# Scores of three batches kept in SBUF, and the state rows' second layer in seven half-block products

## Chip, core and metric

One core of a Trainium2 chip runs the whole kernel. The metric is device time of the launch in microseconds, lower is better. The engines that matter are TensorE (PE in the profile; its weight loads are PEld), VectorE (DVE), ScalarE (ACT), GpSimd (POOL, here only a queue of casting loads) and SyncE (SP, the queue of the stores).

## What is computed

Two blocks follow each other. The first is attention between a sequence and a small state, in both directions; the second is a feed-forward layer with a squared ReLU on every row that the first gives.

```
B, H, S, Ns, D = 8, 8, 512, 32, 64
scores  = scale * x @ state^T          # 512 x 32 for each batch and head
xread   = softmax(scores) @ state      # the sequence reads the state
scores2 = scale * state @ x^T          # the same products, transposed
sread   = softmax(scores2) @ x         # the state reads the sequence
rows    = concat(xread, sread)         # 544 rows per batch, 512 wide
h       = rows @ w_in                  # 512 -> 2048, "layer one"
out     = (s * max(h, 0)^2 + b) @ w_out  # 2048 -> 512, "layer two"
```

So there are 8 x 512 sequence rows and 8 x 32 state rows. The 256 state rows of all batches go through the feed-forward layer together, at the very end.

## The kernel before

**One batch.** `at_xT` (DVE) transposes the batch's rows in 32x32 squares into `xT`. `at_T` (PE) makes the scores `T` of all eight heads in one PSUM tile of two banks (128 partitions x 1024 fp32) with 16 small matmuls that use the array in 32x32 tiles. From `T` two chains start. The first, for the sequence's softmax, is `at_U` (DVE transpose out of PSUM), `at_mu` (maximum), `at_D` (subtract), `at_E1` (exponential on ACT), `at_z`, `at_At`, `at_A`. The second, for the state's softmax, is `at_nm` (DVE maximum of `T`), `at_E2` (two exponentials of `T` on ACT, with their sums), `at_a2`, `at_a2T` (a transpose through PE, `aps`, and a copy back), `at_V` (PE, into `vps`), `at_srd` (an ACT copy into `srdT`, which gathers the state rows of all batches).

The product with the state is folded into `w_in`: `at_M` makes `M = state @ w_in` per batch in four units of 512 columns (`mps`), `at_Mc` copies each to SBUF. Layer one is then `M` against `A`, two matmuls for each of the 16 slices of 128 hidden columns (`layer1_x`, PSUM tile `hps`, two buffers), followed by ReLU on ACT and a square on DVE (`square`, two slices at a time) into `g`. Layer two is `g` against `w_out`.

**The order** is written out by hand: the program does not reorder anything, and each engine executes its list in the order of the calls. A piece for the first batch and a half stands as straight code (L583 to L671). Then come eight calls of `phase`, for b = 0 to 7. Phase b runs layer one of batch b+1 (in phase 7: of the state rows, `sr`) in 16 steps, and layer two of batch b among them. Lists `before` and `behind` hold pairs of a step number and a piece of work that goes ahead of or behind that step's layer one. `chain(b+2, ...)` puts the first softmax chain of the batch after next there.

For batches 3 to 7 both chains start from one `T`. For batches 0, 1 and 2 the first chain has to run early, in the straight code and in phase 0; the second runs late: `late(2, ...)` in phase 3, `late(0, ...)` and `late(1, ...)` in phase 6. Each `late` begins with a second `at_T` of the same batch. (Batch 0 makes its first `T` in two halves of the sequence, in two PSUM tiles, and each half has its own `at_U`.) For that the `xT` of batches 0 to 2 is kept in buffers of their own; the other batches share one.

**Layer two of batches 6 and 7** (`fast_layer2`) is split in 2x2 blocks and done with seven block products in place of eight: DVE makes sums of blocks of `g` (S1 to S4, in place or in `S3`) and, once for the kernel, differences of blocks of `w_out` (`T1` to `T4` of `weight_sum`). The PSUM tile X collects four products and is read out (`evict`) between them; Y holds one, W two. A product is two pieces of eight matmuls of 256 columns, u = 0 to 13, one per step, with step 8 left free: u = 13 stands at step 14, the last eviction and its four DMAs (`put`) behind step 15.

**The end** is layer two of the 256 state rows: 128 rows in 16 matmuls of 512 columns, evicted and stored as one; then the other 128 rows in two halves of 16 matmuls of 256 columns, each evicted (L821) and stored (L824). Both halves lie in one PSUM bank.

In PSUM (eight banks) there are four pairs of banks: `pt` and `pa` (tiles of two banks, shared by `T`, `mps`, `aps`, `vps` in turn), `ph` for layer one and `po` for layer two.

Of the kernel before, what the change touches and what calls it, by code (L numbers as in the profile page):

```python
# [15 lines left out]
def kernel(  # L16
# [12 lines left out]
    nc = tc.nc  # L29
# [138 lines left out]
    def w_out_f(f):  # L168
        return w_out16[:, f, :]
# [58 lines left out]
    def at_xT(b, g=None, p=None):  # L228

        if "xT" not in at[b]:  # L230
            keep = b < 3
            at[b]["xT"] = (konst if keep else apool).tile(
                [P, NG, S, 2], FP16, name=f"xT_{b}", tag=f"xTk{b}" if keep else "xT"
            )
        out = at[b]["xT"].rearrange("p g s e -> p g (s e)").bitcast(FP32)
        in_ = xh_t[b].rearrange("p g j d -> p g (j d)").bitcast(FP32)
        nc.vector.transpose(part(out, p, g), part(in_, p, g))  # L237

    def at_T(b, p=None):

        half = p is not None
        at[b]["T"] = T = two_banks(f"T_{b}", own=not p)
        for e in range(2):
            for hp in range(4):
                for g in range(NG):
                    r = hp ^ g
                    mm(
                        part(T[Ns * hp : Ns * hp + Ns], p, g)[:, 0, :],
                        stE[32 * r : 32 * r + 32, NG * b + g, :, e],
                        part(at[b]["xT"][32 * r : 32 * r + 32, :, :, e], p, g)[:, 0, :],  # L250
                        start=(e == 0), stop=(e == 1),
                        tp=(32 * r, Ns * hp),
                    )

    def at_U(b, p=None, g=None):
        U = sm(b, "U", [P, NG, S], FP32)
# [48 lines left out]

    def at_nm(b):
        nm, nms = sm(b, "nm", [P, NG], FP32), sm(b, "nms", [P, NG], FP32)
        nc.vector.tensor_reduce(  # L308
            nm, at[b]["T"], AX.X, ALU.max, negate=True
        )  # L310
        nc.vector.tensor_scalar(nms, nm, scale, None, ALU.mult)  # L311

    def at_E2(b, gs=range(NG)):
        E2, rs = sm(b, "E2", [P, NG, S], FP16), sm(b, "rs", [P, NG], FP32)
        for g in gs:
            nc.scalar.activation(  # L316
                E2[:, g], at[b]["T"][:, g], AF.Exp,
                bias=at[b]["nms"][:, g : g + 1], scale=scale, accum_out=rs[:, g : g + 1],
            )

# [61 lines left out]
        at_Mc(b, j, copy)  # L382


    G_t, R_t = {}, {}

    def new_G(tag, ntok):
        if tag not in G_t:
            G_t[tag] = gpool.tile([P, NKF, S], FP16, name=f"g_{tag}", tag="g")[:, :, :ntok]
        return G_t[tag]  # L390

    def layer1(tag, f, terms, ntok):
# [78 lines left out]
        }[name]()  # L471
        nc.vector.tensor_sub(T[name], a, b)

    def fast_layer2(b):
# [47 lines left out]
        def put(i, rr):  # L522
# [11 lines left out]
            ("W", lambda: A(0, 1), orig(1, 1), False, True),  # L534
            ("X", lambda: A(1, 1), summed("T4"), False, True),
        ]
        out = [(u + u // 8, lambda u=u: product(*products[u // 2], u % 2)) for u in range(14)]
        out += [(0, lambda: s3(1)), (0, lambda: s1(1)), (1, lambda: evict(top, 0, "X")), (1, lambda: s2(0))]
        out += [(2, lambda: s2(1)), (3, lambda: evict(top, 0, "Y", True))]
        out += [(5, lambda: s4(0)), (6, lambda: evict(top, 1, "X")), (6, lambda: s4(1))]  # L540
# [8 lines left out]
        return [lambda: s3(0), lambda: s1(0)], out  # L549

    def spread_scalars():
        sps = two_banks("sbps")[:, 0, 0:2]
# [121 lines left out]
    def phase(tag, before, behind):  # L674
        for i in range(NKF):
            for when, piece in before:
                if when == i:
                    piece()
            if tag == "sr":
                layer1_sr(i)  # L680
            else:
                layer1_x(tag, i)
            if i and i % 2 == 0:
                square(tag, i - 2)
            for when, piece in behind:
                if when == i:
                    piece()
        square(tag, NKF - 2)

    def chain(b, s):  # L690
        return [
# [60 lines left out]
    for b in range(0, B):  # L752
        if b in fast:
            before, behind = [], fast[b]
        else:
            before, behind = l2(b, 3 if b == 1 else 0) if b else ([], first())
        if b in (2, 4):
            for i, name in enumerate(("T1", "T2") if b == 2 else ("T3", "T4")):
                before += [(12 + 2 * i + h, lambda h=h, name=name: weight_sum(name, h)) for h in range(2)]
        behind = left + behind  # L760
        if b + 1 in FAST:
            sums, fast[b + 1] = fast_layer2(b + 1)
            before += [(14 + i, p) for i, p in enumerate(sums)]
        if b + 3 < B:
            before += [(2 if b else 5, lambda b=b: load_x(b + 3))]
        if b + 3 < B:
            before += [(13, lambda b=b: at_xT(b + 3))]
        if b and b + 2 < B:
            before += [(7, lambda b=b: load_xn(b + 2))]
        if b == B - 3:  # L770
            before += [(9, lambda: load_xn(0))]
        if b == B - 2:
            before += [(4, lambda: load_xn(1))]
        if b == 3:
# [33 lines left out]
    out_sr = out_BSn[:, S:ST, :].rearrange("b (r t) n -> r t b n", r=2)  # L808
    for q in range(4):
        layer2("sr", 0, q)  # L810
    store("sr", 0, out_sr[0:1])
    ops = ps_o.tile([P, DM], FP32, name="ops_sr_1", tag="po")
    osb = opool.tile([P, DM], FP32, name="osb_sr_1", tag="osb")
    for part in range(2):
        sl = slice(DM // 2 * part, DM // 2 * part + DM // 2)
        for f in range(NKF):
            nc.tensor.matmul(  # L817
                ops[:, sl], G_t["sr"][:, f, P:], w_out_f(f)[:, sl],
                start=(f == 0), stop=(f == NKF - 1),
            )  # L820
        nc.vector.scalar_tensor_tensor(  # L821
            osb[:, sl], ops[:, sl], s_bc, bias_bc[:, sl], ALU.mult, ALU.add
        )
        nc.sync.dma_start(out_sr[1][:, :, sl], osb[:, sl])  # L824


# [28 lines left out]
```

## Time and profile before

| | |
|---|---|
| median of three runs | 230.06 us (228.4 to 230.11) |
| profiled execution, its own time | 229.42 us |
| its span, first to last instruction | 227.6 us |
| PE busy | 216.7 us, 95% |
| DVE busy | 175.1 us, 77% |
| ACT busy | 137.0 us, 60% |
| the 16 DMA engines | 22.40 MB, mean 98 GB/s |

Times in the text are those of the trace, counted from the span's start; 1.82 us of the execution's own time lie around its span. PE is busy from about 21 us to the end with hardly a gap. Stretches of it: up to 16 us the first attention chain, while the weights arrive; to 35 us the rest of the straight code; phase 0 to about 54 us; phases 1 to 5 to 173 us; phase 6 to 197 us; phase 7 to 216 us; then the last layer two. A matmul's duration in a row is from its start to its modelled end and overlaps the next; the chain that ended last gives the pitch, and the text uses that.

### The profile page before, as it was taken

The numbers are of one execution on the slowest core, as the hardware profiler recorded it, in microseconds if no ns is written. First come the engines' busy times: TensorE is split into PE (matmuls) and PEld (weight loads), VectorE is DVE, ScalarE is ACT, GpSimd is POOL, SyncE is SP. The second block draws the span as 40 slices with busy tenths as digits, with TensorE's granted clock in tenths as the row PEclk, the third lists the DMA queues.
The fourth block names the chain that finished last, engine by engine and source line by source line (L and its number), as shares of the span: only waits on it lengthen the run. The fifth ranks groups of instructions, "written<-read, shape, count | busy, mean of one in ns | idle before, by whom it ended". The sixth has DMA issues, their size and how long they took to land.

```text
span 227.6 us, 4506 instructions
## 1 busy us (share of the span) xinstructions
PE 216.7 (95%) x1831; PEld 111.4 (49%) x1831; DVE 175.1 (77%) x268; ACT 137.0 (60%) x235; POOL 35.1 (15%) x65
## 2 busy tenths in 40 slices
PE   6597999999999999999999999999999999999982
PEld 2254334443444444444444535444544767788852
DVE  2688997887997598968896589969955996885430
ACT  2277676683797668757876478657866746423300
POOL 8431000106001500063002610030000400000000
PEclk9799999999999999999999999999999999999999
DMA  7999990724932862389527590437042610530272
GB/s 163 195 206 205 207 153 9 150 73 80 160 90 46 117 117 46 71 123 172 97 49 138 93 172 21 93 55 115 17 92 45 82 17 0 116 72 3 49 152 76
DMA packets 22920, 22.40 MB, mean 98 GB/s; under 512 B 4084, under 2 KB 16628, under 8 KB 22900
## 3 DMA queue, kind: packets, MB, share of 16 engines
q0 software_dynamic: 16640, 12.52, 38.1%
q1 hardware_dynamic: 5584, 9.44, 17.2%
q8 instruction: 14, 0.23, 0.4%
q10 hardware_dynamic: 676, 0.16, 0.3%
q14 instruction: 6, 0.05, 0.1%
HBM read 25.72 MB, written 8.91 MB: 152 GB/s over the span
## 4 chain that ended last, share of the span: by engine, by line
PE 86%; DMA 7%; DVE 3%; POOL 2%; issue 1%; ACT 0%; POOLq 0%
PE ops L433 35%; PE hps L395 24%; DMA w_in<-in_moe_w_in_dram 7%; PE opf_X L74 6%; PE mps L74 4%; PE hps_sr L395 3%; PE opf_W L74 3%; PE T L74 3%; PE vps L74 2%; PE ops_sr L817 2%; PE aps L74 2%; PE opf_Y L74 2%; PE ops_sr L433 2%; POOL xh L117 1%; POOL w_in L132 1%
## 5 line engine op out<-in xcount | busy, mean ns | idle before, releaser
L433 PE MATMUL ops<-w_out,g 128*128 128x512 f16 x384 | 97.9, 379 | 0.9 <-DMA w_out<-in_moe_w_out_dram 0.9
L398 ACT ACTIVATE r<-hps 128x512 f16<-128x512 f32 x120 | 71.0, 606 | 30.9 <-PE hps L395 30.3
L395 PE MATMUL hps<-A,M 128*128 128x512 f16 x240 | 70.2, 381 | 0.2 <-ACT r L398 0.2
L433 PEld LDWEIGHTS <-g 128*128 128x128 f16 x384 | 37.5, 98 | 46.0 <-issue 1.1
L403 DVE TENSOR_TENSOR g<-r 128x1024 f16<-128x1024 f16 x60 | 40.9, 682 | 15.9 <-ACT r L398 15.8
L395 PEld LDWEIGHTS <-M 128*128 128x128 f16 x240 | 20.8, 98 | 27.4 <-issue 8.7
L378 ACT CAST M<-mps 128x1024 f16<-128x1024 f32 x31 | 31.3, 1010 | 2.5 <-PE mps L74 2.3
L126 POOL DMA_DIRECT2D xn<-in_x_dram x32 | 18.5, 588 | 51.2 <-PE vps L74 50.3
L74 PEld LDWEIGHTS <-g 128*128 128x128 f16 x192 | 18.7, 98 | 4.8
L443 DVE SCALAR_TENSOR_TENSOR osb<-ops,sb_bc,bias_bc 128x512 f32<-128x512 f32 x24 | 17.9, 746 | 1.2 <-PE ops L433 1.2
L316 ACT ACTIVATE E<-T,nms 128x512 f16<-128x512 f32 x16 | 11.0, 687 | 5.7 <-DVE nms L311 5.7
L114 POOL COPY ahead<-xT 1x2 f16<-1x2 f16 x5 | 1.2, 250 | 84.0 <-DVE xT L237 68.1
L398 ACT ACTIVATE r_sr<-hps_sr 128x256 f16<-128x256 f32 x16 | 6.1, 383 | 13.0 <-PE hps_sr L395 12.9
L274 ACT ACTIVATE E<-Dm 128x1024 f16<-128x1024 f32 (+1 forms) x9 | 8.7, 963 | 8.6 <-DVE Dm L267 8.5
L257 DVE STREAM_TRANSPOSE U<-T 128x1024 f32<-128x1024 f32 (+1 forms) x9 | 10.1, 1124 | 3.4 <-PE T L74 3.4
L279 DVE TENSOR_REDUCE z<-E 128x32 f32<-128x1024 f16 (+1 forms) x9 | 9.9, 1099 | 2.8 <-ACT E L274 2.6
L237 DVE STREAM_TRANSPOSE xT<-xh 128x1024 f32<-128x1024 f32 (+2 forms) x12 | 10.2, 872 | 1.7 <-DMA xh<-in_x_dram 1.7
L74 PE MATMUL mps<-w_in,stT 64*32 64x512 f16 x256 | 11.2, 390 | 0.3 <-DMA w_in<-in_moe_w_in_dram 0.3
L360 ACT CAST srdT<-vps 128x128 f16<-128x128 f32 x8 | 5.7, 775 | 8.8 <-PE vps L74 8.8
L267 DVE TENSOR_TENSOR Dm<-U,mu 128x1024 f32<-128x1024 f32 (+1 forms) x9 | 9.9, 1100 | 0.1
L261 DVE TENSOR_REDUCE mu<-U 128x32 f32<-128x1024 f32 (+1 forms) x9 | 9.8, 1090 | 0.0
L308 DVE TENSOR_REDUCE nm<-T 128x2 f32<-128x1024 f32 x8 | 9.7, 1218 | 0.0
(76 smaller groups left out, 215.6 us busy)
## 6 DMA issues: line engine op xcount, KB each, us to landing
out_dram<-osb SPq DMA_DIRECT2D x40, 128.0 KB, 3.6
xn<-in_x_dram POOLq DMA_DIRECT2D x32, 128.0 KB, 6.3
xh<-in_x_dram POOLq DMA_DIRECT2D x15, 256.0 KB, 4.8
w_in<-in_moe_w_in_dram POOLq DMA_DIRECT2D x4, 512.0 KB, 12.8
w_out<-in_moe_w_out_dram POOLq DMA_DIRECT2D x4, 512.0 KB, 17.6
out_dram<-osx SPq DMA_DIRECT2D x16, 128.0 KB, 2.4
out_dram<-osb SPq DMA_DIRECT2D x4, 256.0 KB
xf<-in_x_dram SPq DMA_DIRECT2D x1, 512.0 KB, 3.5
```

Source lines behind the costliest of these rows:

```text
L74: return nc.tensor.matmul(out, lhsT, rhs, start=start, stop=stop, tile_position=tp, is_transpose=is_transpose, skip_group_check=skip,)
L126: nc.gpsimd.dma_start(out=xn_t[b][32 * jh : 32 * jh + 32].rearrange("t h c d -> t h (c d)"), in_=x[b].rearrange("h (t jh c) d -> jh t h (c ...
L237: nc.vector.transpose(part(out, p, g), part(in_, p, g))
L257: nc.vector.transpose(part(U, p, g), part(at[b]["T"], p, g))
L267: nc.vector.tensor_tensor(blk(part(Dm, p, g)), blk(part(at[b]["U"], p, g)), over_n(part(at[b]["mu"], p, g)), ALU.subtract,)
L316: nc.scalar.activation(E2[:, g], at[b]["T"][:, g], AF.Exp, bias=at[b]["nms"][:, g : g + 1], scale=scale, accum_out=rs[:, g : g + 1],)
L378: copy(at[b]["M"][:, :, 512 * j : 512 * j + 512], at[b]["mps", j])
L395: nc.tensor.matmul(hps, lhsT, rhs, start=(i == 0), stop=(i == len(terms) - 1))
L398: nc.scalar.activation(R_t[tag, f - f % 2][:, f % 2], hps, AF.Relu)
L403: nc.vector.tensor_mul(new_G(tag, r.shape[2])[:, f : f + 2], r, r)
L433: nc.tensor.matmul(ops_t[tag, rr], G_t[tag][:, f, P * rr : P * rr + P], w_out_f(f), start=(f == 0), stop=(f == NKF - 1),)
L443: nc.vector.scalar_tensor_tensor(osb, ops_t.pop((tag, rr)), s_bc, bias_bc, ALU.mult, ALU.add)
```

## The change

The scores of batches 0, 1 and 2 are copied from PSUM to SBUF by ACT (`at_keep`, tile `Ts`, fp32) when they are first made, and the second chain of these batches reads the copy. The second `at_T` goes. All batches share the one `xT` buffer.

Layer two of the state rows becomes the same scheme of seven block products, with blocks of 128 rows and 256 output columns; the sums lie in the unused half of `g`'s buffer. The sums of the first half of the hidden slices are put at steps 10 to 13 of phase 7, the others between the evictions at the end. X, Y and W are three PSUM tiles of their own.

Some pieces move by a step: E1 of batch 2 and its first two M units in phase 0 (10 to 11), the last product piece of `fast_layer2` (14 to 15), for batch 7 its last eviction and four DMAs (behind the first product of the end), `late(1, ...)` (nm from 7 to 6, V from 12 to 13), and the last square of phase 7 (ahead of the last product piece of step 15).

```diff
     def at_xT(b, g=None, p=None):
         if "xT" not in at[b]:
-            keep = b < 3
-            at[b]["xT"] = (konst if keep else apool).tile(
-                [P, NG, S, 2], FP16, name=f"xT_{b}", tag=f"xTk{b}" if keep else "xT"
-            )
+            at[b]["xT"] = apool.tile([P, NG, S, 2], FP16, name=f"xT_{b}", tag="xT")
...
+    def at_keep(b, p=None):
+        if "Ts" not in at[b]:
+            at[b]["Ts"] = konst.tile([P, NG, S], FP32, name=f"Ts_{b}")
+        act(part(at[b]["Ts"], p), part(at[b]["T"], p))
...
     def at_nm(b):
-        nc.vector.tensor_reduce(
-            nm, at[b]["T"], AX.X, ALU.max, negate=True
-        )
+        T = at[b].get("Ts", at[b]["T"])
+        nc.vector.tensor_reduce(nm, T, AX.X, ALU.max, negate=True)
...
-                E2[:, g], at[b]["T"][:, g], AF.Exp,
+                E2[:, g], at[b].get("Ts", at[b]["T"])[:, g], AF.Exp,
...
-        out = [(u + u // 8, lambda u=u: product(*products[u // 2], u % 2)) for u in range(14)]
+        out = [(u + u // 8 + u // 13, lambda u=u: product(*products[u // 2], u % 2)) for u in range(14)]
...
-            (15, lambda: evict(low, 0, "X")),
-            (15, lambda: put(1, 0)), (15, lambda: put(1, 1)),
+            (end, lambda: evict(low, 0, "X")),
+            (end, lambda: put(1, 0)), (end, lambda: put(1, 1)),
...
     at_T(0, 0)
     T0 = at[0]["T"]
+    at_keep(0, 0)
     at_xT(0, 1, 1)
     at_xT(0, 0, 1)
     at_T(0, 1)
+    at_keep(0, 1)
...
     layer1_half(0, 6, 1)
+    at_keep(1)
     layer2(0, 1, 0)
...
     def late(b, s):
         return [
-            (s[0], lambda: at_T(b)),
             (s[1], lambda: at_nm(b)),
...
-            s = (1, 2, 3, 3, 4, 4, 5, 6, 7, 8, 9) if b else (5, 6, 7, 8, 9, 8, 9, 10, 11, 12, 13)
+            s = (1, 2, 3, 3, 4, 4, 5, 6, 7, 8, 9) if b else (5, 6, 7, 8, 9, 8, 9, 11, 11, 12, 13)
+            before += [] if b else [(6, lambda: at_keep(2))]
...
-            plan = [(2, 0, [(1, 3)]), (10, 0, [(2, 0), (2, 1)])]
+            plan = [(2, 0, [(1, 3)]), (11, 0, [(2, 0), (2, 1)])]
...
-            before += late(0, (1, 2, 3, 4, 5, 6, 7)) + late(1, (6, 7, 8, 9, 10, 11, 12))
+            before += late(0, (1, 2, 3, 4, 5, 6, 7)) + late(1, (6, 6, 8, 9, 10, 11, 13))
+        if b == B - 1:
+            before += [(10 + i, lambda name=name: sum_sr(name, 0)) for i, name in enumerate(("S1", "S2", "S3", "S4"))]
...
+    product_sr(X, A_sr(0, 0), w_block(0, 0), first=True)
+    sum_sr("S1", 1)
+    sum_sr("S2", 1)
+    evict_sr(0, 0, X, False)
+    for when, piece in fast[B - 1]:
+        if when == NKF:
+            piece()
+    product_sr(Y, A_sr(0, 1), w_block(1, 0), first=True, last=True)
+    sum_sr("S3", 1)
+    evict_sr(0, 0, Y, True, True)
+    product_sr(X, S_sr("S2"), w_sum("T2"))
+    evict_sr(0, 1, X, False)
+    sum_sr("S4", 1)
+    product_sr(W, S_sr("S1"), w_sum("T1"), first=True)
+    evict_sr(1, 1, W, False)
+    product_sr(X, S_sr("S3"), w_sum("T3"))
+    evict_sr(1, 1, X, True, True)
+    product_sr(W, S_sr("S4"), w_block(1, 1), last=True)
+    evict_sr(0, 1, W, True, True)
+    product_sr(X, A_sr(1, 1), w_sum("T4"), last=True)
+    evict_sr(1, 0, X, True)
```

`product_sr` issues eight matmuls of 256 columns, one for each pair of hidden slices; `evict_sr` scales, adds the bias (or, with True, what an earlier eviction wrote) on DVE, and with a last True starts a DMA of 128 KB. `sum_sr(name, h)` is one DVE sum of 128x512 fp16.

More of the change, by code (lines that the diff above doesn't have):

```diff
@@ L382, in at_M2 @@
         at_Mc(b, j, copy)
-    G_t, R_t = {}, {}
+    G_t, R_t, whole_t = {}, {}, {}
     def new_G(tag, ntok):
         if tag not in G_t:
-            G_t[tag] = gpool.tile([P, NKF, S], FP16, name=f"g_{tag}", tag="g")[:, :, :ntok]
+            whole_t[tag] = gpool.tile([P, NKF, S], FP16, name=f"g_{tag}", tag="g")
+            G_t[tag] = whole_t[tag][:, :, :ntok]
         return G_t[tag]
@@ L472, in weight_sum, with fast_layer2 @@
         nc.vector.tensor_sub(T[name], a, b)
-    def fast_layer2(b):
+    def fast_layer2(b, end):
         S3 = konst.tile([P, NKF // 2, HALF], FP16, name=f"S3_{b}", tag="S3")
@@ L545, in fast_layer2, with sr_block, S_sr, sum_sr @@
             (13, lambda: put(0, 0)), (13, lambda: put(0, 1)),
-            (15, lambda: evict(low, 0, "X")),
-            (15, lambda: put(1, 0)), (15, lambda: put(1, 1)),
+            (end, lambda: evict(low, 0, "X")),
+            (end, lambda: put(1, 0)), (end, lambda: put(1, 1)),
         ]
         return [lambda: s3(0), lambda: s1(0)], out
+    out_sr = out_BSn[:, S:ST, :].rearrange("b (r t) n -> r t b n", r=2)
+    def sr_block(i, j):
+        return whole_t["sr"][:, j::2, P * i : P * i + P]
+    def S_sr(name):
+        i = int(name[1]) - 1
+        return whole_t["sr"][:, NKF // 2 * (i % 2) : NKF // 2 * (i % 2 + 1), 2 * P + P * (i // 2) : 3 * P + P * (i // 2)]
+    def sum_sr(name, h):
+        A = sr_block
+        x, y, op = {
+            "S1": (A(1, 0), A(1, 1), ALU.add),
+            "S2": (S_sr("S1"), A(0, 0), ALU.subtract),
+            "S3": (A(0, 0), A(1, 0), ALU.subtract),
+            "S4": (A(0, 1), S_sr("S2"), ALU.subtract),
+        }[name]
+        out, x, y = (t[:, 4 * h : 4 * h + 4] for t in (S_sr(name), x, y))
+        nc.vector.tensor_tensor(out, x, y, op)
+    def w_block(j, n):
+        return lambda k: w_out_f(2 * k + j)[:, HALF * n : HALF * n + HALF]
+    def w_sum(name):
+        return lambda k: fast_w[name][:, k]
     def spread_scalars():
@@ L684, in phase @@
                 square(tag, i - 2)
+            if i == NKF - 1 and tag == "sr":
+                square(tag, i - 1)
             for when, piece in behind:
@@ L687, in phase @@
                     piece()
-        square(tag, NKF - 2)
+        if tag != "sr":
+            square(tag, NKF - 2)
     def chain(b, s):
@@ L761 @@
         if b + 1 in FAST:
-            sums, fast[b + 1] = fast_layer2(b + 1)
+            sums, fast[b + 1] = fast_layer2(b + 1, NKF - 1 if b + 2 < B else NKF)
             before += [(14 + i, p) for i, p in enumerate(sums)]
@@ L805, with product_sr, evict_sr @@
             out_x(b, 3)
[L808 to L820, printed above, removed]
+    X, Y, W = two_banks("ops_sr_X", own=True), two_banks("ops_sr_Y"), ps_o.tile([P, HALF], FP32, name="ops_sr_W", tag="po")
+    X, Y = X[:, 0, :HALF], Y[:, 0, :HALF]
+    def product_sr(ps, lhsT, rhs, first=False, last=False):
+        for k in range(NKF // 2):
+            mm(ps, lhsT[:, k], rhs(k), start=(first and k == 0), stop=(last and k == NKF // 2 - 1), skip=True)
+    def evict_sr(i, n, ps, last, plus=False):
+        sl = slice(HALF * n, HALF * n + HALF)
         nc.vector.scalar_tensor_tensor(
-            osb[:, sl], ops[:, sl], s_bc, bias_bc[:, sl], ALU.mult, ALU.add
+            osr[i][:, sl], ps, s_bc, osr[i][:, sl] if plus else bias_bc[:, sl], ALU.mult, ALU.add
         )
-        nc.sync.dma_start(out_sr[1][:, :, sl], osb[:, sl])
+        if last:
+            nc.sync.dma_start(out_sr[i][:, :, sl], osr[i][:, sl])
+    osr = [opool.tile([P, DM], FP32, name=f"osr_{i}", tag="osb") for i in range(2)]
+    A_sr = sr_block
+    product_sr(X, A_sr(0, 0), w_block(0, 0), first=True)
[19 more added lines that the diff above has]
+    evict_sr(1, 0, X, True)
 _INS = ['x', 'state', 'moe_w_in', 'moe_w_out', 'moe_s', 'moe_b']
```

## The prediction

> **What bounds the kernel.** I read the busy times first, then the chain that ended last, as shares of the span by engine.
>
> ```profile
> PE 216.7 (95%) x1831; PEld 111.4 (49%) x1831; DVE 175.1 (77%) x268; ACT 137.0 (60%) x235; POOL 35.1 (15%) x65
> ...
> PE 86%; DMA 7%; DVE 3%; POOL 2%; issue 1%; ACT 0%; POOLq 0%
> ```
>
> PE is busy and is also what everything waits for: 86% of the chain, the 7% of DMA being the weights' arrival up to 20.7 us. So work taken from PE after 21 us shortens the span by PE's own pitch, unless DVE or ACT come late in its place. The same chain in order of time gives that pitch. The second `at_T` of batch 2, and those of batches 0 and 1 (two of the last one's records are missing):
>
> ```profile
> 114.87 0.57 PE T L74 x16
> ...
> 174.40 0.57 PE T L74 x16
> ...
> 182.79 0.57 PE T L74 x14
> ```
>
> Then the end of the chain, with one product piece of `fast_layer2` ahead of it:
>
> ```profile
> 208.06 0.87 PE opf_X L74 x8
> ...
> 215.92 3.45 PE ops_sr L433 x16
> 219.37 1.76 PE ops_sr L817 x16
> 221.13 0.03 issue
> 221.16 0.49 DVE osb_sr L821
> 221.66 0.04 issue
> 221.70 1.92 PE ops_sr L817 x16
> 223.62 0.03 issue
> 223.64 0.48 DVE osb_sr L821
> ```
>
> The reader is to see 7.13 us of matmuls (3.45 + 1.76 + 1.92), a hole of 0.57 (221.13 to 221.70) in which PE waits for the eviction because both halves share a bank, and 3.5 us from the last eviction's start to the span's end (a DMA). The timeline of the start:
>
> ```profile
> 7.26 0.62 ACT L589 CAST xh<-xf 128x512 f16<-128x512 f32 x1
> ...
> 8.76 0.68 DVE L257 STREAM_TRANSPOSE U<-T 128x512 f32<-128x512 f32 x1
> ...
> 10.92 0.63 ACT L274 ACTIVATE E<-Dm 128x512 f16<-128x512 f32 x1 [3.04 <-DVE Dm L267]
> ...
> 18.17 1.02 PE L433 MATMUL ops<-w_out,g 128*128 128x512 f16 x4 [0.89 <-DMA w_out<-in_moe_w_out_dram]
> ```
>
> ACT has 3.04 us free there, and PE waits for weights at 18.17 (0.89 us) and again at 20.75 (0.35).
>
> **1. The second scores go.** Three times 0.57 on the chain: **-1.71**. What is late next? Phase 3 has slack: DVE and ACT wait for PE there. In phase 6 DVE has no idle between 176.4 and 188.0. I followed its list there with PE 0.57, then 1.14 earlier. X's second eviction ends 2.9 us before PE needs it; the S2 sums end 1.1 us before theirs. The tightest are the two steps of batch 1's late chain: `a2` ends at 189.60 and its transposes start at 189.70; `a2T` ends at 191.46 and V starts at 191.55. The change moves nm of batch 1 ahead of one square and one eviction, 1.3 us up DVE's list, and V one step (1.3 us) down PE's, which pays for the 1.14. Without those moves the missed cover would cost up to 1.1. I take 0, ends 0 and +0.6.
>
> **2. The copies.** Four on ACT, two of 128x512 and two of 128x1024, fp32 to fp32 from PSUM: no row has this form. Nearest: stT<-sps 0.59 and 1.03, M<-mps 1.01, ReLU 0.60. I take 0.6 and 1.0. None is a gain in itself; what matters is who waits.
> - Batch 0: in the changed program each U waits for the copy ahead of it, although both only read. T is done at 8.66, ACT is free from 7.88, so the copy runs 8.7 to 9.3 and U starts 0.56 later; U, mu, D and E1 move by 0.56 (E1 to 11.5), A of the first half from 14.03 to 14.6. PE runs dummy matmuls until 14.56, so layer one starts only about 0.05 later, and the weights' waits of 0.89 and 0.35 take that in. **0**; if those covers were gone, up to two times 0.6, that is +1.2. [...]
> - Batch 1: here the copy waits for U (ends 23.06) and for ACT (23.39), so 23.4 to 24.4; the two ReLUs behind it start at 24.4 in place of 24.04. Their next user on PE comes at 26.44, behind a weights' wait. 0.
> - Batch 2, phase 0: U ends at 42.58, the copy runs 42.6 to 43.6 and holds the ReLUs of slices 6 and 7 to 44.15 and 44.7. Layer one has two PSUM buffers; slice 9 would start at 44.65: a stall of 0.1. Then ACT has E1 and two M copies. In the old order PE waited for ReLUs at 49.6 and 51.4 (0.07 and 0.2); with E1 behind slice 10's ReLU and M one step later these waits go, but E1 ends 0.3 later and with it DVE's list to the square of slices 14 and 15 (ends 54.91, wanted at 55.47, and now PE is earlier by 0.3). Sum: +0.1 - 0.27 + about 0.1: **0**, ends -0.3 and +1.2 (the whole copy and a bit).
>
> **3. Sources and buffers.** nm read PSUM in 1.22; mu reads SBUF in the same 1.21. E2 0.69 against E1's 0.63 for a half from SBUF. Neither is on the chain: 0. The one `xT`: batch 1 writes it at 19.2 (batch 0's last reader ended at 9.4), batch 2 at 38.0 (21.7), batch 3 at 51.2 (41.3; GpSimd's small read 39.5). At least 9.8 us of cover each: 0; without it a wait on DVE of that reader's length, 0.6.
>
> **4. The end on PE.** Seven products of eight matmuls of 256 columns, each 0.87 by the opf row: 6.09 in place of 7.13, and no hole if evictions keep ahead: -1.04 - 0.57 = **-1.61**. u = 13 only changes place with slice 15's layer one, so the first new product starts at 215.92 like the old one; W of batch 7 and X of the end are other banks than those still being read.
>
> **5. The end on DVE.** New there: seven evictions of 128x256 (0.48 by L821), four sums of 128x512 (0.43 by the square of g_sr), and the old eviction of batch 7 (0.75) which came before 216.3. In the list's order, from the square of slices 14 and 15 (done 215.95): S1, S2 to 216.8; X's first eviction 216.8 to 217.3 (product 3 may start at 217.66); batch 7's eviction to 218.0; S3 to 218.4; Y's eviction to 218.85; X's second, product 3 being done at 218.53, to 219.3, product 5 wants it at 219.40: 0.05 to spare; S4; W's to 220.13 (wanted 220.27); X's third 220.3 to 220.8 (wanted 221.14); W's last; X's last from 222.04. So no stall, but by a hair. If a sum took 0.68 (the dearest two-input sum here, for twice the elements), DVE would be up to 0.25 late at each of four and PE would stall up to 0.8. The four earlier sums of phase 7 (1.7 us) fall where DVE is busy 12.2 of 19 us: 0.
>
> **6. Stores.** Batch 7's last four DMAs of 128 KB are issued from 218.0, 0.63 apart (8 in 5.08 before), then four of the end: 220.5, 221.1, 221.75 and, behind the last eviction, 222.55. The DMA share stood at 0.96 with 209 GB/s while such DMAs followed each other (215.5 to 216.5), 0.63 us for each 128 KB, so the queue just empties before the last; 0, ends 0 and +0.6 (one DMA ahead of it).
>
> **Sum**: -1.71 - 1.61 + 0 = -3.3; 229.42 - 3.3 = 226.1 on the profiled execution's own scale. The median of the three runs lies 0.64 higher, one run 1.0 lower; I forecast **226.3**, 1.6% below the median. Its own range: 225.2 to 227.5 (both gains, the spread of the runs, small stalls).
>
> **Rivals.**
> A. The end becomes DVE's: sums at 0.68 or waits of some 0.1 at each of five hand-overs; 0.8 to 1.6 of the 1.61 is lost. Time 227.1 to 227.9. For: DVE has 0.05 us to spare at product 5. Against: the square of the same size takes 0.43.
> B. The copies count: +0.6 to +1.8 from the start and phase 0. For: U waits, ACT runs dense from 46.7 to 52.8. Against: the weights' waits. Time 226.9 to 228.2.
> C. Slower: at the end PE and DVE take turns instead of overlapping, as they did in the hole at 221.13. Seven products with an eviction after each, 7 x (0.87 + 0.03 + 0.48 + 0.04) = 9.9, with the sums and batch 7's eviction between (1.7 + 0.75) 12.4 us where 215.92 to 224.12 took 8.2: +4.2 - 1.7 = +2.5, time 232. It decides as soon as each product waits for the eviction just before it. Against: between two products in X lies one in Y or W, in another bank.
> D. The change does not take its gain: the second `at_T` hides nothing and is gone for certain, but phase 6 may become DVE's, which leaves -0.6 of its -1.14: 226.9.
>
> Chances: forecast 0.68, A 0.11, B 0.11, C 0.05, D 0.05. From 225.2 to 228.4 all but C and the outermost misses of both sides are held: that is the range. About 1% (2.3 us, 227.8) is what a measurement of this kernel tells from no change. Faster by over 1%: nearly all of the forecast and D and half of A and B: 0.78. Within 1%: 0.16. Slower: C and a little unknown, 0.06.
>
> **What would show it.** The scores' group on PE falls from 192 to 144 matmuls, with an ACT copy row of four. U of batch 0 starts near 9.3, yet PE's wait for w_out at 18.2 stays. Phase 7 starts 1.7 earlier (phase 6's end 197 to 195.3 and the last layer two 215.9 to 214.2); less says B or D. From there to the last eviction's start 6.1 in place of 7.7; more, with PE waiting for osr evictions, says A or C. A last DMA landing over 3.7 us after the last eviction's start says step 6 was wrong. A wait in the straight code that is not the weights', or a new one on `ph` in phase 0, would make the whole wrong upward.

## The result, and the profile after

| | before | after |
|---|---|---|
| median of four runs each, side by side | 229.53 us (228.4 to 230.11) | 226.36 us (225.35 to 227.9) |
| ratio of the times | | 0.9879, 95% interval 0.9842 to 0.9916 |
| profiled execution, its own time | 229.42 us | 225.35 us |
| its span | 227.6 us | 223.6 us |

The changed kernel is 1.2% faster: 226.36 us where 226.3 was forecast. The page of the changed kernel, busy times and the shares of the chain that ended last:

```profile
PE 213.3 (95%) x1791; PEld 111.5 (50%) x1791; DVE 179.6 (80%) x280; ACT 139.7 (62%) x239; POOL 35.0 (16%) x65
...
PE 87%; DVE 6%; DMA 3%; ACT 2%; issue 1%; POOLq 0%
```

PE lost 3.4 us of busy time and 40 matmuls (48 of the scores gone, 8 added at the end), DVE and ACT gained 4.5 and 2.7, and PE carries the chain as before. The larger share of DVE and the smaller one of DMA come almost wholly from the start, where the chain of this execution runs through DVE's list instead of the weights. The chain that ended last, in order of time, at the end of the changed kernel (start us, us, what):

```profile
212.60 0.87 PE opf_X L74 x8
213.47 0.87 PE ops_sr_X L74 x8
214.35 0.87 PE ops_sr_Y L74 x8
215.22 0.87 PE ops_sr_X L74 x8
...
218.71 0.89 PE ops_sr_X L74 x8
219.60 0.03 issue
219.63 0.48 DVE osr L855
```

The seven products follow each other with no hole: 6.16 us from 213.47 to the last eviction's start, where the old end took 7.72 (215.92 to 223.64). The last eviction starts 3.97 us before the span's end, 3.96 before. The same stretch on DVE, from the timeline:

```profile
214.79 0.74 DVE L521 SCALAR_TENSOR_TENSOR osx<-opf_X,sb_bc,bias_bc 128x512 f32<-128x512 f32 x1
215.44 0.41 DVE L573 TENSOR_TENSOR g_sr<-g_sr 128x512 f16<-128x512 f16 x1
215.78 0.47 DVE L855 SCALAR_TENSOR_TENSOR osr<-ops_sr_Y,sb_bc,osr 128x256 f32<-128x256 f32 x1
216.17 0.47 DVE L855 SCALAR_TENSOR_TENSOR osr<-ops_sr_X,sb_bc,bias_bc 128x256 f32<-128x256 f32 x1
...
219.63 0.48 DVE L855 SCALAR_TENSOR_TENSOR osr<-ops_sr_X,sb_bc,bias_bc 128x256 f32<-128x256 f32 x1 [0.39 <-PE ops_sr_X L74]
```

X's second eviction ends at 216.64. Product 5 stands at 216.97 in the chain, 0.33 us later; but the chain counts it from the end of product 4, and its first matmul starts at 216.80 in the timeline, so DVE is really 0.16 us ahead there. A sum takes 0.41, an eviction 0.47 to 0.48; but the next instruction starts 0.39 after an eviction's start, and 0.65 after the start of the 0.74 one.

Now the account, piece by piece, from the pitch of the two chains:

| | forecast | in the two profiled executions |
|---|---|---|
| up to the scores of batch 1 (21.09, now 20.74) | 0 | -0.35 (of it -0.26 from the rows' arrival: first T at 8.24, now 7.98) |
| from there to the scores of batch 2 (19.5 us in both) | 0 | 0.00 |
| phase 0 | 0 | -0.06 |
| the three second scores | -1.71 | -2.03 (0.67, 0.67, 0.69) |
| the end on PE | -1.61 | -1.56 |
| stores | 0 | +0.01 |
| sum | -3.3 | -4.0 |

The profiled execution gained 4.0 and the median 3.2. Two things were to be explained: why a group of 0.57 us saves 0.68, and why the executions of the changed kernel lie so far apart (225.35 to 227.9).

### The profile page after: what moved, and what is told of

The parts are those of the page before. It is cut to its first block, busy times and chain, and to the rows that moved or that the text cites. A ratio compares the mean times of both kernels' runs of the same rounds, so it can differ in the third digit from the quotient of the medians.

```text
span 223.6 us, 4445 instructions
## 1 busy us (share of the span) xinstructions
PE 213.3 (95%) x1791; PEld 111.5 (50%) x1791; DVE 179.6 (80%) x280; ACT 139.7 (62%) x239; POOL 35.0 (16%) x65
## 4 chain that ended last, share of the span: by engine, by line
PE 87%; DVE 6%; DMA 3%; ACT 2%; issue 1%; POOLq 0%
PE ops L436 36%; PE hps L398 24%; PE opf_X L74 6%; PE mps L74 4%; PE opf_W L74 3%; PE hps_sr L398 3%; DMA xh<-in_x_dram 3%; PE vps L74 2%; PE T L74 2%; PE aps L74 2%; PE ops_sr_X L74 2%; PE opf_Y L74 2%; DVE U L260 1%; DVE Dm L270 1%; DVE mu L264 1%
## 5 line engine op out<-in xcount | busy, mean ns | idle before, releaser
L318 ACT ACTIVATE E<-T,nms 128x512 f16<-128x512 f32 x10 | 6.9, 687 | 4.3 <-DVE nms L313 4.3
L398 PE MATMUL hps_sr<-srdT,w_in 128*128 128x256 f16 x64 | 9.3, 273 | 0.0
(86 smaller groups left out, 226.1 us busy)
```

Source lines behind the costliest of these rows:

```text
L398: nc.tensor.matmul(hps, lhsT, rhs, start=(i == 0), stop=(i == len(terms) - 1))
```

## The experiments

All ratios are to the kernel before on the same chip. A kernel's time behind its start is counted here as its span less the moment at which the scores of batch 1 start: 206.5 us before and 202.86 after. Since it is the same in every profiled execution of one kernel (202.84 and 202.81 in two further ones of the changed kernel), the span of an unprofiled execution tells when its start was over.

### The change again, and its two parts

The changed kernel was run once more. "Scores only" takes back the new end; "sr only" takes back the copies and keeps the new end.

```diff
 scores only, against the changed kernel
-    def fast_layer2(b, end):
+    def fast_layer2(b):
...
-            whole_t[tag] = gpool.tile([P, NKF, S], FP16, name=f"g_{tag}", tag="g")
...
-            before += [(10 + i, lambda name=name: sum_sr(name, 0)) for i, name in enumerate(("S1", "S2", "S3", "S4"))]
```

```diff
 sr only, against the changed kernel
-    at_keep(0, 0)
-    at_keep(0, 1)
-    at_keep(1)
...
+            (s[0], lambda: at_T(b)),
```

> The changed kernel once more, beside its parts. The prediction's sum is -3.3 us against before, the trace of the changed kernel showed -4.0 in its span, of which 0.35 lay ahead of 40 us, where the weights arrive. If those 0.35 belong to the change (theory W), they show again: the first layer two in the straight code starts near 17.6 in place of 18.2. If they are the scatter of the weights' arrival from execution to execution (rival), the start of that matmul differs from 17.6 by some tenths here and in the other runs, whichever kernel it is. Time: 3 to 4 us below before.

> The copies, the shared buffer and the moves that go with them; layer two of the state rows as before. By the prediction's step 1: three times 0.57 = -1.71 us. Rival from the two traces: each second set of scores also made the layer-one pair behind it 0.54 long in place of 0.43, so three times 0.68 = -2.04 us, read at the start of the last layer two. The last eviction starts 7.7 us after that, as before.

> The seven products at the end and the moved last pieces of layer two of batches 6 and 7; the scores are made twice as before. By steps 4 to 6: -1.61 us, all of it behind the start of the last layer two (7.72 to 6.11 us from there to the last eviction's start) and nothing ahead of it. Rival A would leave 0 to -0.8 of it, rival C +4. The sum of this run's gain and that of the scores alone should be that of both, within the intervals.

| | median | ratio, 95% interval | span of the profiled execution | scores of batch 1 at | behind the start |
|---|---|---|---|---|---|
| the change again | 225.82 | 0.9860 (0.9825 to 0.9894) | 224.1 | 21.26 | 202.84 |
| scores only | 228.67 | 0.9974 (0.9953 to 0.9995) | 226.3 | 21.83 | 204.5 |
| sr only | 227.53 | 0.9929 (0.9909 to 0.9948) | 226.3 | 21.39 | 204.9 |

The end alone is worth 0.71% of 229.22, that is 1.63 us, and 1.6 in the trace: step 4's size. The scores alone are worth 2.0 us behind the start (206.5 less 204.5), yet only 0.6 us of the median. The two parts add up behind the start (-2.0 and -1.6 against -3.65). What the scores lose lies ahead of 22 us. Of twelve executions of "scores only" one has its start over before 21 (span 224.9, less 204.5 gives 20.4), the other eleven between 21.5 and 23.0. Without the copies ("sr only" and the kernel before, 52 executions) it is 19.9 to 21.8. The changed kernel and four of the runs below do the same work in the same order up to there, and they are late less often: after 21.5 in 8 of the changed kernel's 16 executions and in 3 of the others' 16. Why "scores only" is late in eleven of twelve stays open.

In its second profile the changed kernel started the first layer two at 17.17, in its third at 19.24, where the first had 17.63. So its 0.35 us ahead of batch 1's scores are scatter from execution to execution and no part of the gain.

### What one group of scores costs

Three products of the scores' form that nobody reads (extra work) are put back where the second scores stood.

```diff
         if b == 3:
+            before += [(10, lambda: at_extra(5))]
...
         if b == B - 2:
+            before += [(1, lambda: at_extra(7)), (6, lambda: at_extra(7))]
```

> The changed kernel with three sets of scores made once more at the old places (into a tile that nobody reads, from the transposed rows at hand), so that PE has its old work and the copies stay. If a set costs its own pitch alone: 3 x 0.57 = +1.71 us against the changed kernel. If it also costs the change of the array's tiling, which the trace shows as 0.11 on the layer-one pair behind it: 3 x 0.68 = +2.04. In the chain: pairs of layer one at 0.54 behind the first two sets, and 0.11 more on the transposes behind the third, which here stand between it and layer one.

Measured 227.06 us, ratio 0.9920 (0.9891 to 0.9950), and 204.9 us behind the start: +2.04 for three groups, 0.68 each. The chain that ended last of this kernel, and then, of the changed kernel, the stretch where that group is missing:

```profile
172.80 0.87 PE opf_X L74 x8
173.67 0.57 PE Tx L74 x15
174.25 0.54 PE hps L412 x2
```

```profile
173.32 0.43 PE hps L398 x2
173.75 0.87 PE opf_X L74 x8
174.62 0.64 PE vps L74 x32
175.26 0.54 PE hps L398 x2
...
176.67 0.43 PE hps L398 x2
```

The layer-one pair takes 0.43, but 0.54 when it stands directly behind a group in small tiles (T in 32x32, V in 128x64, and M in 64x32, whose pair in the changed kernel's chain takes 0.54 at 142.47). The group itself takes 0.57; the other 0.11 is lost by the matmuls that follow it. If that is so, a group put directly behind another group of small tiles costs 0.57 only, because the pair behind is slow already:

```diff
         if b == 3:
+            before = [(6, lambda: at_extra(5))] + before
...
         if b == B - 2:
+            before += [(2, lambda: at_extra(7)), (7, lambda: at_extra(7))]
```

> The changed kernel with three products of the scores' form added that nobody reads (extra work), as in the run that put them back alone, but each directly behind another group of small tiles (an M product or a V product) instead of between full matmuls. If a removed group saved 0.57 of its own and 0.1 that the full matmul pair behind a group of small tiles loses (0.54 in place of 0.43): the pair behind is already slow, so 3 x 0.57 = 1.71, and 202.86 + 1.71 = 204.6 us from batch 1's scores to the end. If the group of 16 matmuls itself costs 0.68: 2.04, and 204.9.

The chain of this kernel:

```profile
175.14 0.64 PE vps L74 x32
175.78 0.57 PE Tx L74 x15
176.35 0.54 PE hps L412 x2
```

The scores of batch 1 start at 20.68 and the end's first product at 214.97, so 194.29 us lie between them where the changed kernel has 192.57 (20.74 to 213.31): +1.72 where 1.71 was expected of this and 2.04 of the rival. (One execution, 227.0 us.) The loss of 0.11 stands at the return from small tiles to the full array, on the layer-one pair behind the group (0.54 in place of 0.43); the group itself takes 0.57 behind full matmuls and behind V alike, and whether a part of that is the way into its tiling is not shown.

### The copies of phase 0, and the moved pieces

Each copy on ACT is done twice (extra work):

```diff
         act(part(at[b]["Ts"], p), part(at[b]["T"], p))
+        act(part(at[b]["Ts"], p), part(at[b]["T"], p))
```

> Each copy is made twice, so ACT spends 3.2 us more. By step 2: in the start U moves by another 0.6, layer one from 14.6 to 15.2, of which the weights' waits take all but some 0.3; batch 1's copies end at 25.4 and their ReLUs at 26.5, just when PE wants them: 0; in phase 0 the ReLUs of slices 6 and 7 move by 1.0 and PE stalls by about 1.0. Sum +1.3 over the changed kernel. Theory S: the start alone adds 1 to 2 us in most executions, with scores of batch 1 at 22 to 23; sum +2 to +3. If ACT had hidden slack everywhere: 0.

Measured 228.76, ratio 0.9963 (0.9938 to 0.9987). From the scores of batch 2 to those in phase 1 it took 16.39 us in place of 15.32: +1.07 for one more copy of 1.02. The chain that ended last, in phase 0 of this kernel:

```profile
42.91 1.26 DVE U L261
44.17 0.02 issue
44.19 1.02 ACT Ts L256
45.21 0.02 issue
45.24 1.02 ACT Ts L257
46.25 0.51 ACT r L402
46.76 0.04 issue
46.80 1.08 PE hps L399 x4
```

So the first copy (1.02) is hidden and the second is not: ACT there has room for about one copy and no more. The profiled span is 3.6 us longer in all (227.15 less 223.57): 1.95 more lie in the start again (batch 1's scores at 22.69), and 0.6 behind the last eviction, where this one execution took 4.5 us from its start to the span's end and the thirteen others 3.9 to 4.0.

Then the moved pieces of phase 0 and phase 6 went back to their old steps, with everything else as changed:

```diff
-            s = (1, 2, 3, 3, 4, 4, 5, 6, 7, 8, 9) if b else (5, 6, 7, 8, 9, 8, 9, 11, 11, 12, 13)
+            s = (1, 2, 3, 3, 4, 4, 5, 6, 7, 8, 9) if b else (5, 6, 7, 8, 9, 8, 9, 10, 11, 12, 13)
...
-            plan = [(2, 0, [(1, 3)]), (11, 0, [(2, 0), (2, 1)])]
+            plan = [(2, 0, [(1, 3)]), (10, 0, [(2, 0), (2, 1)])]
...
-            before += late(0, (1, 2, 3, 4, 5, 6, 7)) + late(1, (6, 6, 8, 9, 10, 11, 13))
+            before += late(0, (1, 2, 3, 4, 5, 6, 7)) + late(1, (6, 7, 8, 9, 10, 11, 12))
```

> The changed kernel with E1 and the M units of batch 2 at step 10 of phase 0 and the late chain of batch 1 in its old steps. By step 1 the cover of that chain would be missed by up to 1.1 us in phase 6 (transposes or V waiting for DVE); by step 2 phase 0 gains or loses 0.3. So 0 to +1.4. Rival: DVE's list in phase 6 has more room than its idle time tells, and the moves do nothing: within 0.2 in the trace from the start of phase 6 (172.4) to the last layer two (213.5).

Phase 6 took 22.95 us in place of 22.26, phase 0 15.85 in place of 15.32. The chain that ended last runs through DVE in phase 6 from 174.47 to 189.57 (but for 2 us of ACT behind the second nm), and V waits for its input:

```profile
188.30 0.66 DVE osx L521
188.96 0.61 DVE a2T L339
189.57 0.04 issue
189.62 0.69 PE vps L74 x31
```

Without the moves 0.69 of the gain of phase 6 is gone, and 0.53 in phase 0. In the times the 1.2 us don't show (226.51, ratio 0.9887, 0.9848 to 0.9926): the starts of these executions differ by more.

### DVE at the end

The sums made between the evictions are done twice, four more of 0.43 us (extra work):

```diff
+    sum_sr("S1", 1)
+    sum_sr("S2", 1)
...
+    sum_sr("S3", 1)
...
+    sum_sr("S4", 1)
```

> The changed kernel with each of the four sums that stand at the end made twice, 1.7 us more for DVE. The prediction left DVE 0.05 us to spare at product 5, so each second sum ahead of it is a stall: the two second sums ahead of X's first eviction move it by 0.8, product 3 is late by 0.45 and with the next sums the end by 1.2 to 1.6. The trace of the changed kernel shows shorter pitches (evictions 0.39 in place of 0.48) and 0.3 to spare at product 5: then the end is late by 0.5 to 1.2. Rival A is true if nothing of the two holds and the end moves by the whole 1.7 or more.

Measured 226.86, ratio 0.9905 (0.9868 to 0.9942). From the end's first product to the last eviction's start it took 7.64 us (215.54 to 223.18) in place of 6.16: +1.48 of the 1.7 added. PE's timeline has what rival A spoke of:

```profile
217.81 1.03 PE L74 MATMUL ops_sr_X<-w_T,g_sr 128*128 128x256 f16 x8 [0.54 <-DVE osr L855]
...
220.05 1.03 PE L74 MATMUL ops_sr_X<-w_T,g_sr 128*128 128x256 f16 x8 [0.33 <-DVE osr L855]
...
221.24 1.03 PE L74 MATMUL ops_sr_W<-w_out,g_sr 128*128 128x256 f16 x8 [0.15 <-DVE osr L855]
```

So at the end DVE has some 0.2 us of slack in the changed kernel, and all that was added beyond it came out as time.

### The start: three orders of the same work

In the start U waits for the copy ahead of it, as forecast (timeline of the changed kernel; in brackets the idle time before and what ended it):

```profile
8.68 1.24 ACT L256 COPY Ts<-T 128x512 f32<-128x512 f32 x2 [1.67 <-PE T L74]
...
9.29 0.72 DVE L260 STREAM_TRANSPOSE U<-T 128x512 f32<-128x512 f32 x1 [0.71 <-ACT Ts L256]
...
11.33 0.41 PE L74 MATMUL mps<-w_in,stT 64*32 64x512 f16 x8
...
12.14 0.38 PE L74 MATMUL sbps<-sb_one,ones 1*128 1x2 f32 x2 [0.40 <-DVE U L260]
12.45 1.04 PE L610 MATMUL dps<-ones 128*128 128x512 f16 x4
...
14.65 1.03 PE L74 MATMUL hph<-A,M 128*128 128x256 f16 x8
```

What the forecast did not have is the fourth line. `spread_scalars`, a product of two columns (`sbps`), takes the pair of banks in which U's second half is read, so it waits for U, and with it all that PE has behind it: here a hole of 0.40 us. The first remedy puts the copies of batch 0 behind U and behind E1:

```diff
-    at_keep(0, 0)
     at_xT(0, 1, 1)
     at_xT(0, 0, 1)
     at_T(0, 1)
-    at_keep(0, 1)
     T1, at[0]["T"] = at[0]["T"], T0
     at_U(0, 0)
+    at_keep(0, 0)
...
     at_E1(0, 0)
+    at_keep(0, 1)
```

> The changed kernel with the two copies of batch 0 behind the transposes: U of the first half, then its copy; U of the second half, E1 of the first, then the second copy. So no transpose waits for a copy. The first four runs leave this open: the spans of kernels without the copies, less what follows the scores of batch 1 (206.5 us before, 204.9 with the seven products alone), put those scores at 20.1 to 21.4 us; with the copies they stand at 20.1 to 23.0. Theory S: the copy ahead of U makes PE wait for U in the start (0.4 to 1.4 us at the small scalar product), it then runs longer at half clock, and in some executions layer one starts late by more than the weights' waits cover. Then here the scores stand at 20.1 to 21.4 again, spans of 223.0 to 224.3, a median about 0.3 us under that of the changed kernel (224.05). Rival, step 2 of the prediction: the covers hold, the scatter is the chip's; spans spread 223.0 to 225.7 as in the changed kernel, no difference of medians.

Measured 225.29 us (225.13 to 225.61), ratio 0.9824 (0.9805 to 0.9843), with spans of 223.3 to 223.8. Those four lie close together; the profiles of the slower starts in the other runs suggested the next experiment. PE is at half pace where its dummy matmuls take 0.47 us each in place of 0.26 (the duration of a group over its number). Where the small product was held up inside such a stretch, half pace went on for longer. Three kernels were therefore run side by side: the changed one, the one with the copies behind U, and the changed one with the copies where they are but the same twelve dummies divided otherwise, so that PE is busy instead of waiting for U:

```diff
-    idle(5)
+    idle(7)
     at_M2(0, 0, True)
     spread_scalars()
-    idle(4)
+    idle(3)
...
-    idle(3)
+    idle(2)
```

> The changed kernel once more, unchanged, so that its executions and those of the order with the copies behind U stand beside each other on one chip. If the copies ahead of U cost the start 0 to 2 us from execution to execution: a median near 225.8, times spread over 224.8 to 227.5. If the spread seen before came from that chip or that moment: within 0.5 us of the other order, and as narrow.

> The order with batch 0's two copies behind U once more. If the start is what it repairs: 225.1 to 225.7, 0.4 to 0.6 below the changed kernel's median and with less than 1 us between the fastest and the slowest undisturbed execution. If its narrow times were chance: a median of 225.8 and executions of 227 among them.

> The changed kernel with the copies of batch 0 still ahead of U, but the same twelve dummy matmuls divided 7, 3 and 2 in place of 5, 4 and 3, so that TensorE is busy up to the small scalar product instead of idle while that one waits for U. Theory G (the hole of 0.4 to 0.8 us in TensorE's stream, in the stretch in which it runs at half pace, is what prolongs that stretch): the half pace ends by 12.5 us as in the kernel before, layer one starts by 14.9, the scores of batch 1 by 21.2, times 225.1 to 225.9 without any of 227. Theory U (the vector chain behind the late U sets the start, whatever TensorE does meanwhile): as the changed kernel, batch 1's scores between 20.1 and 23.2, a median of 225.8. Rival to both: the two dummies ahead (0.43 each at half pace) hold up the small scalar product and M by up to 0.4 where there was no long hole: 0.1 to 0.4 worse than the changed kernel in its fast starts.

| | median | ratio, 95% interval | all spans |
|---|---|---|---|
| changed | 226.85 | 0.9873 (0.9836 to 0.9909) | 223.3, 223.4, 224.9, 225.2, 225.5, 226.1 |
| copies behind U | 225.81 | 0.9821 (0.9799 to 0.9844) | 222.9, 223.2, 224.0, 224.1, 225.4 |
| hole filled | 225.12 | 0.9819 (0.9799 to 0.9839) | 222.8, 223.2, 223.3, 224.0, 224.2 |

PE's timeline of the changed kernel in this run's profiled execution, and then of the one with the hole filled:

```profile
11.26 0.63 PE L74 MATMUL mps<-w_in,stT 64*32 64x512 f16 x8
11.96 0.58 PE L74 MATMUL sbps<-sb_one,ones 1*128 1x2 f32 x2
12.48 1.89 PE L610 MATMUL dps<-ones 128*128 128x512 f16 x4
...
16.11 1.57 PE L74 MATMUL hph<-A,M 128*128 128x256 f16 x8
```

```profile
8.32 3.17 PE L610 MATMUL dps<-ones 128*128 128x512 f16 x7
11.42 0.52 PE L74 MATMUL mps<-w_in,stT 64*32 64x512 f16 x8
11.87 0.38 PE L74 MATMUL sbps<-sb_one,ones 1*128 1x2 f32 x2
12.18 0.82 PE L610 MATMUL dps<-ones 128*128 128x512 f16 x3
...
13.49 0.60 PE L610 MATMUL dps<-ones 128*128 128x512 f16 x2
13.93 1.04 PE L74 MATMUL hph<-A,M 128*128 128x256 f16 x8
```

In the first the dummies behind the small product take 0.47 each and layer one begins at 16.11; in the second they take 0.27 and it begins at 13.93. All profiled executions, sorted by whether the small product met half pace (M's first product takes 0.63 instead of 0.41) and how far it starts behind M's first product, 0.56 being the pitch of an unbroken stream at half pace. The first T starts when the batch's rows have arrived, between 7.1 and 8.4 whatever the kernel, so the last column counts from there:

| | M's first product | small product behind it by | dummies behind it, each | layer one at | first T at | from it to the scores of batch 1 |
|---|---|---|---|---|---|---|
| half pace, not held: before | 0.63 | 0.56 | 0.26 | 14.58 | 8.24 | 12.85 |
| sr only | 0.63 | 0.56 | 0.37 | 15.30 | 8.38 | 13.01 |
| no moves | 0.63 | 0.56 | 0.26 | 13.92 | 7.46 | 12.55 |
| three products beside small tiles | 0.63 | 0.55 | 0.42 | 14.58 | 7.13 | 13.55 |
| hole filled | 0.52 | 0.45 | 0.27 | 13.93 | 7.32 | 12.70 |
| half pace, held: scores only | 0.63 | 1.45 | 0.47 | 15.47 | 7.37 | 14.46 |
| copies twice | 0.63 | 1.12 | 0.47 | 16.16 | 7.25 | 15.44 |
| sums twice | 0.63 | 0.70 | 0.47 | 16.44 | 8.13 | 14.65 |
| changed, third run | 0.63 | 0.70 | 0.47 | 16.11 | 7.81 | 14.88 |
| copies behind U, again | 0.63 | 0.70 | 0.47 | 16.41 | 8.11 | 14.47 |
| full pace already, held: changed | 0.41 | 0.81 | 0.26 | 14.65 | 7.98 | 12.76 |
| changed, again | 0.41 | 1.77 | 0.26 | 14.02 | 7.56 | 13.70 |
| three products put back | 0.41 | 0.91 | 0.26 | 14.31 | 7.64 | 12.76 |
| copies behind U | 0.41 | 0.70 | 0.26 | 14.41 | 7.97 | 12.60 |

All five executions in which the hold-up fell within half pace took 14.5 to 15.4 us, the other nine 12.6 to 13.7. (In "no moves" and with the hole filled half pace ended at 11.47 and 11.69, before or just as the small product started; so three profiles show it passing unheld through half pace.) In the third group PE was held up for as long or longer, and layer one still began by 14.65. The chain behind the late U, which theory U makes responsible, is there too: in the changed kernel's chain the copy (8.68, 0.59) and U (9.29, 0.73) stand one behind the other on the way to layer one. But it costs little: 12.76 against 12.60 with the copies behind U. And with the hole filled U waits for the copy as before (0.50 us) and the start takes 12.70. So the 2 us go with the hole together with the pace (theory G), not with U's being late. The rival to both, that the two dummies put ahead cost 0.1 to 0.4, did not come either: the other division also takes two dummies from behind the small product.

What remains with less than certainty: the ratios of the three kernels touch each other's intervals, so that the remedies are faster than the changed kernel rests on the profiles and on the spread (7 of the changed kernel's 16 executions in all have a span above 224.5, one of 9 with the copies behind U, none of 5 with the hole filled), and the last has one profile only. Run again, the copies behind U came out as their expectation had it for chance: a median of 225.81 and one execution of 227.19. They only shorten the hold-up: the small product then waits for the second copy, and one profile of two still shows the late start. Both remedies together were not run.

## Why the prediction was right, and where not

**Step 1** failed in size: 0.57 was the group's own time, and the term should have been 0.68 a group, because with each group goes one return to the full array (0.11). The row was in the trace of before, one line below the quoted ones (174.97, `hps` 0.54); the term counted only the group's line. What it said of cover was right: phase 6 did not become DVE's with the moves, and without them it lost 0.69 where "up to 1.1" was given.

**Step 2** was right for batch 1 (0.00), for phase 0 (-0.06, and one copy more costs +1.07, close to the upper end of 1.2 that "the whole copy and a bit" stood for) and for the copies' length (0.585 and 1.02 against 0.6 and 1.0). For batch 0 it followed U, mu, D, E1 and A to layer one, and U came at 9.29 as forecast. But it did not name the one instruction of PE that waits for U itself, the small product, and did not ask what a hole does to PE's pace. That the weights' waits take the delay in then held in some executions and not in others: 0 to 2 us, with layer one up to 16.4 where 14.6 was forecast. PE's wait for w_out stayed in the profiled execution, with 0.27 at 17.63 in place of 0.89 at 18.17. The profile names DVE's z as what ended it, because z ends just then; but layer two doesn't read z, and GpSimd's next load, which the landing of w_out releases, follows 0.24 us later in both kernels (17.87 and 18.41). This much of rival B, the copies that count, was true, from the start alone and not from phase 0. U waits 0.71 for the copy although both only read, and placed behind U the copy waits for it (it starts at 9.42, U runs from 8.67 to 9.39); no run lets the two read at once, so what would happen then is not shown. The order of those two reads is what opens the hole.

**Step 3** held: the chain shows no wait of a new `xT` for a reader of the old one, and no longer nm or E2 that anything waits for.

**Step 4** was right: -1.56 in the trace and -1.63 in the times of the end alone, for -1.61. The hole of 0.57 is gone: Y's product starts at 214.18 in the timeline, and X's first eviction runs from 214.38 to 214.86 beside it. That PE waited at 221.13 because the halves shared a bank was the author's reading; they shared a tile as well, and no run separates the two.

**Step 5** had the right verdict with too little spare: 0.33 us instead of 0.05 at product 5 by the chain's count (0.16 to its first matmul), because evictions were laid end to end at 0.48 while DVE starts the next after 0.39. Its list was also added up short: with its own prices X's second eviction ends at 219.43, 0.03 after product 5 wants it, and not 0.05 before. The doubled sums show that rival A was 0.2 us away from being true. Rival C (turns of PE and DVE, 232) did not come, since no product waits for the eviction just before it.

**Step 6** was right to 0.01, but read the row of before wrongly: from the last eviction's start to the span's end it is 3.96 us before and 3.97 after; 3.5 is counted from the eviction's end. Its sign of being wrong, "over 3.7 us", rests on that row and tells nothing.

So the sum of -3.3 came out by two misses that nearly cancel: 0.32 too little for the scores, and too little for the start, where executions differ by more than 2 us. The forecast 226.3 met the median of 226.36, and the median of all 16 runs of the changed kernel, 226.1; the rest of the working, not that number, says how good it was.

## What to carry to other kernels

When a group of small-tile matmuls is taken out from between full ones, count the slower matmuls behind it with it (0.11 us a group here); when it is only moved to stand beside another such group, that part alone is gained. When an engine's chain starts later, list everything that waits for its buffers and not only for its results, the small products on PE above all. In a start where PE is at half pace, a wait of a tenth of a microsecond went with a loss of up to 2 us here, so look for such holes, try filling them or moving what opens them, and compare the spread of the executions as well as their median.

## What was not expected of the hardware

**The pace of PE in the start.** Where PE fell back to half pace and nothing interrupted it, it lasted 3.4 us (granted clock 0.50 in the changed kernel from 7.75 to 11.16, before from 9.09 to 12.51), and twice that where it was interrupted (scores only: 9.18 to 16.01). A hold-up of 0.14 us (0.70 against 0.56) went with it as surely as one of 0.9. In seven profiles (the last four of the second group, sr only, and both with three products) the granted clock reads 1.00 there while dummies take 0.42 to 0.47 from the first one on, so that the durations and not that column were used. Idle time alone doesn't decide whether half pace goes on: in the kernel before PE stood idle from 5.04 to 6.33, behind eight dummies of 0.45 each, and the eight products of `sps` that came next took 0.41, where in the changed kernel's third run, with no idle ahead of them, they took 0.64. The small product doesn't stand in that stretch. It stands in the half pace of the five with the late start, with its wait, and of three others without a wait (before, sr only, three products beside small tiles); in those three M's second product is at full pace again (0.41, at 13.58 to 14.30), in the five it is not (0.63, at 13.65 to 14.63). The small product fills two columns and takes 0.54 to 0.58 us of PE's line there; no run leaves it out, and why 0.14 us suffices stays open.

**The return from small tiles**: 0.11 us on the layer-one pair behind each group (0.54 in place of 0.43), shown above.

**DVE's pitch**: an eviction of 128x256 from PSUM shows 0.48 us but the next instruction starts 0.39 to 0.41 after its start; for 128x512 it is 0.74 and 0.65.
